# GpSimd DRAINs in the conditional expert blocks, and x's four buffers moved to 256 bytes (modulo 512) from the weights

## The chip, the core and the metric

The kernel runs on one NeuronCore of a Trainium2 chip. The metric is the device time in microseconds of one execution; the median of three runs is compared. Engines are named as the profile names them: PE is TensorE's matmuls, PEld its weight loads, DVE is VectorE, ACT is ScalarE, POOL is GpSimd, SP is SyncE; a q behind a name (POOLq) marks an instruction that the engine's sequencer runs by itself.

## The reference, cut to what matters

Three stages follow each other on 4608 tokens of 512 features.

```
attn:  8 heads, chunks of 64 tokens: softmax(q k^T / 8) v        -> x    (4608 x 512)
moe:   h = max(x@w1, x@w2, x@w3);  x2 = h @ w_out                 FF 768
moe2:  e = argmax(x2 @ w_gate) for each token, 8 experts
       out = prob(e) * sigmoid(x2 @ w_output_gate)[e] * (relu(x2 @ w1[e]) @ w2[e])   FF 1024
```

All is float32; each product of the dense parts is done as three matmuls of high and low parts (hi·hi, hi·lo, lo·hi).

## The kernel before, in words

**Attention and the dense layer.** The 36 tiles of 128 tokens are cut into nine blocks of four tiles (512 tokens). A planner (`add`, `order`) writes out by hand in which order each engine's instructions stand. Attention of the next block fills the gaps of the current block's dense layer. Attention leaves x transposed, split into a high and a low half, in `xt[j % 2]`: even blocks use the buffers `xth0` and `xtl0`, odd blocks `xth1` and `xtl1`, each 128 partitions of 4·512 floats (8192 bytes). `moe_f` (18 calls a block) multiplies: a weight piece of 128x128 from `wpc` is the stationary operand, 512 columns of `xt` stream past it; `mm3` is the three matmuls, lines 102 (hi, hi), 103 (hi, lo) and 104 (lo, hi), so a block has 18·4·3 = 216 such matmuls. `moe_y` then has `ht` as the stationary and `wo` as the moving operand (256 or 272 columns). `gate` ranks the tokens by expert, and `rows_out` writes x2 to a scratch tensor in HBM.

**The expert stage.** Tokens of one expert are taken in blocks of 256. `step(b)` does one block: `gather_ahead(b + 2)` (POOL: `places`, then two indirect DMAs that gather 128 rows each into `xg`), first layer (`l1_mm`: stationary `wpc`, 256 moving columns of `xs`), the transposes of the next block (`x_T`), second layer (`l2_mm`: stationary `wo`'s `hT`, 512 moving columns of `wpc`), and for each half `y_act` on ACT and `y_out`, an indirect DMA on POOL that scatters 128 rows to the output. Where the next block has another expert, `switch` loads and splits new weights. Blocks 0 to 17 always run; `tail` puts blocks 18 to 25 into nested conditions (`tc.If(total > b)`), since how many are needed depends on the routing. With these inputs blocks 18, 19 and 20 run and 21 to 25 do not. Line 1192 is the condition, and what an engine does at it where the block is left out; line 1232 is the close of the whole program; line 1212 its start.

**Where the buffers lie.** A pool hands out addresses in the order in which its tags are first asked for. In pool `p1` the six small `mx` and `sm` buffers (32 bytes a partition each) come first, then the slots of `xth0`, `xtl0`, `xth1`, `xtl1`, then `ht0` to `ht5`, `hs0`, `U` and the small gate buffers. A slot is as large as the largest tile that uses it: `xth1`'s slot is later used for `xg01` (2·2·516 floats, 8256 bytes), `xtl1`'s slot for `xs0`, `ht`'s slots for `yo`. The pool `wp` with the weights (`wpc` pieces of 16384 and 8192 bytes, then `wo`) stands ahead of `p1`. Within the expert stage `hT` and the odd blocks' `xs` lie in `wo`, at multiples of 512 bytes from the weights.

Of the kernel before, what the change touches and what calls it, by code (L numbers as in the profile page):

```python
# [10 lines left out]
F32 = mybir.dt.float32  # L11
# [10 lines left out]
def tile_chunk_attention_moe_moe(  # L22
# [16 lines left out]
    PE, ACT, DVE, POOL, SP = nc.tensor, nc.scalar, nc.vector, nc.gpsimd, nc.sync  # L39
# [7 lines left out]
    P = 128  # L47
# [5 lines left out]
    XW = DM + 4  # L53
# [3 lines left out]
    NB0 = NT // BP  # L57
# [108 lines left out]
    p1 = ctx.enter_context(tc.tile_pool(name="p1", bufs=1))  # L166

    def buf(shape, dtype, name):
        return p1.tile(shape, dtype, name=name, tag=name)
# [10 lines left out]
    pTF = [part(3, i, 1).rearrange("p (a c i) -> p a c i", a=HP, c=2) for i in range(2)]  # L180
    NV = len(v_buf)
    mxs, sms = ([buf([P, H], F32, f"{n}{i}") for i in range(NE2)] for n in ("mx", "sm"))
    XN = KD * TB * P
    xtn = lambda hl, i: f"xt{'hl'[hl]}{i}"
    xtile = lambda hl, i: p1.tile([P, KD, TB * P], F32R, name=xtn(hl, i), tag=xtn(hl, i))
# [559 lines left out]
    NX = 3  # L745
# [16 lines left out]
    lastx = (NB - 1) % 2  # L762

    def xkeys(i, *hls):
        return [("xt", i, t, hl, h2) for t in range(TB) for hl in hls for h2 in range(2)]
# [5 lines left out]
        [("pTF", i) for i in range(2)] + [("cy", i) for i in range(2)],  # L771
    ]
    raw = [Late(ar, f"R{n}", [P, 4, DM], F32, f"raw{n}", akeys[n]) for n in range(4)]
    xg01 = Late(p1, xtn(0, 1 - lastx), [P, 2, 2, XW], F32, "xg01",
                xkeys(1 - lastx, 0) + [("xg", i, t) for i in range(2) for t in range(2)])
    xs0 = Late(p1, xtn(1, 1 - lastx), [P, 2, KD, BP], F32R, "xs0", xkeys(1 - lastx, 1) + [("xs0", i) for i in range(4)])
    xg2 = Late(wp, f"P{NFT // 4}", [P, 2, XW], F32, "xg2", [("w", n, hl) for n in range(16, NFT) for hl in range(2)])
    S2 = Late(p1, xtn(0, lastx), [P, XN], I32, "S2", xkeys(lastx, 0) + ["S2"])
    yol = [Late(p1, f"ht{i}", [P, DM], F32, f"yo{i}", [("ht", i, 0), ("ht", i, 1)]) for i in range(4)]
# [21 lines left out]
    ]  # L801
    xsk = [[("xs0", i) for i in range(4)], [("wo", i) for i in range(8, 12)]]
    hTk = [("wo", i) for i in range(8)]
    xg = lambda b: xg2.t if b % NX == 2 else xg01.t[:, b % NX]
    yo = lambda b, t: yol[2 * (b % 2) + t].t
    bk = [("mm", 0), ("mm", 1), ("mm", 2), ("mm", 0)]
    ps_x = ps_a2.rearrange("p (a b) -> p a b", a=KD)
# [11 lines left out]
    def sval(engines, row, b, hi):  # L819
        return nc.values_load(  # L820
            sched_i()[0:1, row * NBLK + b:row * NBLK + b + 1], engines=engines, min_val=0, max_val=hi
        )
# [7 lines left out]
    def gather(b, t, rows=NT):  # L830
        POOL.indirect_dma_start(  # L831
            out=xg(b)[:, t], out_offset=None, in_=x2d[0:rows, :],
            in_offset=bass.IndirectOffsetOnAxis(ap=ic[b % 4]()[:, t, 0:1].bitcast(U32), axis=0),
        )

    def places(b):
        cv = sval([ET.Pool], 0, b, NCOL - 2)
        POOL.tensor_copy(ic[b % 4](), idx()[:, bass.ds(cv, 2), :])  # L838
# [18 lines left out]
    def l1_mm(b, c, i):  # L857
        x, ps = xs[b % 2](), l1_ps(c)
        w, ff = wx[c // 2], ((2 * c + i) % 4) * P
        for kk in range(KD):  # L860
            mm3(
                ps[:, i], w[:, 0, kk, ff:ff + P], w[:, 1, kk, ff:ff + P], x[:, 0, kk], x[:, 1, kk],
                kk == 0, kk == KD - 1,
            )

    def l1_hi(c):
        ACT.activation(out=hT()[:, 0, 2 * c:2 * c + 2], in_=l1_ps(c), func=ACTF.Relu)  # L867

    def l1_lo(c):
        fs = slice(2 * c, 2 * c + 2)  # L870
        DVE.scalar_tensor_tensor(  # L871
            out=hT()[:, 1, fs], in0=l1_ps(c), scalar=0.0, in1=f(hT()[:, 0, fs]), op0=ALU.max, op1=ALU.subtract
        )
# [235 lines left out]
    def x_T(b):  # L1109
        if b < NBLK:  # L1110
            xT_mm(b)
            for i in range(2):
                xT_hi(b, i)
                xT_lo(b, i)

    def switch(b, ns):


        lv, cl, en = meta[b]
        with tc.If(lv > 0):  # L1120
            for n in ns:
                for kk in range(4):
                    conv_hi(n, kk)
                    conv_lo(n, kk)
        for n in ns:
            load_x(n, en, cl)

    def scalars(b):
        meta[b] = (
            sval([ET.Activation, ET.DVE], 1, b, 1), sval([ET.SP], 2, b, 1), sval([ET.SP], 3, b, E - 1)  # L1130
        )

    def gather_ahead(b):
        if b < NBLK:
            places(b)
            for t in range(2):
                gather(b, t)

    def l2(b, t):
        for ff in range(2 * KD):  # L1140
            l2_mm(t, ff)
        if t == 0:
            y(b, t)

    def y(b, t):
        y_act(b, t)
        y_out(b, t)

    def step(b):
        scalars(b)  # L1150
        gather_ahead(b + 2)
        for c in range(4):
            for i in range(2):
                l1_mm(b, c, i)
            l1_hi(c)
            l1_lo(c)
            if c == 2:
                switch(b, (0,))
        x_T(b + 1)
        switch(b, (1,))  # L1160
        if b + 1 < NBLK:
            full[b + 1] = sval([ET.PE], 7, b + 1, 1)
        l2(b, 0)
        with tc.If(full[b] > 0):
            l2(b, 1)
        y(b, 1)
        switch(b, (2, 3))
# [17 lines left out]
    for b in range(1, NB0):  # L1185
        step(b)
    total = sval(None, 6, 0, NBLK)

    def tail(b):
        if b == NBLK:  # L1190
            return
        with tc.If(total > b):  # L1192
            step(b)
            tail(b + 1)
# [42 lines left out]
```

## Time and profile before

| | |
|---|---|
| median of three runs | 1209.3 us (1208.03 to 1210.64) |
| the profiled execution | 1207.82 us, span 1206.0 us from the first to the last instruction |
| PE busy | 1181.2 us, 98% of the span |
| DVE, ACT, POOL busy | 436.7, 418.1, 195.7 us |
| granted TensorE clock | 0.995 of full speed over the span |

Busy time is a share of the span; matmuls are pipelined and their ends modelled, so a busy PE may still run at different rates. The rate is read from start to start of matmuls that follow each other. Sequencer instructions (branches, semaphore waits, DRAIN) do not count as busy and stand in the view of a source line alone.

### The profile page before, as it was taken

What the parts mean: (1) busy time and instruction counts of PE and PEld (TensorE: products, weight loads), DVE (VectorE), ACT (ScalarE), POOL (GpSimd) and SP (SyncE); (2) the same over time, 40 slices, a digit from 0 to 9 for tenths busy, and PEclk for the clock granted to TensorE, in tenths of its full rate; (3) what the DMA queues carried; (4) which work ended last, traced back from release to release, by engine and by line L of the source; (5) the groups of instructions that cost most, each with busy time, mean ns of one, the idle gap of its engine ahead of it and who ended that gap; (6) DMA issues with size and microseconds to landing.
All of it is one profiled execution on the core that took longest, in us unless ns stands there. A gap on an engine that the chain in (4) does not pass through costs nothing. (4 is left out here: it accounts for less than half of the span.)

```text
span 1206.0 us, 23510 instructions
## 1 busy us (share of the span) xinstructions
PE 1181.2 (98%) x9219; PEld 1035.3 (86%) x9219; DVE 436.7 (36%) x1095; ACT 418.1 (35%) x1192; POOL 195.7 (16%) x243
## 2 busy tenths in 40 slices
PE   7999999999999999999999999999999999999995
PEld 6879788897888988988879898989989989999994
DVE  7995413232232322322323452211266211511270
ACT  5575323333243332333322322212256212512271
POOL 1000111111211111111111112112112212112120
PEclk9999999999999999999999999999999999999998
DMA  8842212121121121211230015111156211511151
GB/s 283 245 140 71 86 30 87 47 58 59 35 80 53 47 69 36 80 54 35 73 106 36 1 45 201 54 45 53 46 207 241 100 44 48 180 45 62 38 171 29
DMA packets 84318, 103.06 MB, mean 85 GB/s; under 512 B 40287, under 2 KB 49503, under 8 KB 84192
## 3 DMA queue, kind: packets, MB, share of 16 engines
q1 hardware_dynamic: 77152, 79.82, 20.7%
q0 software_dynamic: 7040, 21.60, 5.6%
q8 instruction: 75, 1.23, 0.4%
q14 instruction: 51, 0.42, 0.1%
HBM read 149.55 MB, written 20.52 MB: 141 GB/s over the span
## 5 line engine op out<-in xcount | busy, mean ns | idle before, releaser
L102 PE MATMUL mm<-xth,wpc 128*128 128x512 f32 x576 | 233.8, 406 | 0.0
L104 PE MATMUL mm<-xth,wpc 128*128 128x512 f32 x576 | 226.5, 393 | 0.0
L103 PE MATMUL mm<-xtl,wpc 128*128 128x512 f32 x576 | 226.0, 392 | 0.1
L613 DVE TENSOR_TENSOR hs<-mm,hs 128x512 f32<-128x512 f32 x108 | 74.4, 688 | 184.0 <-PE mm L104 184.0
L871 DVE SCALAR_TENSOR_TENSOR wo<-mm,wo 128x512 fp32r<-128x512 f32 x64 | 43.5, 689 | 239.1 <-ACT wo L867 208.6
L104 PEld LDWEIGHTS mm<-xth,wpc 128*128 128x128 f32 x576 | 108.3, 188 | 24.7
L102 PEld LDWEIGHTS mm<-xth,wpc 128*128 128x128 f32 x576 | 108.2, 188 | 23.8
L103 PEld LDWEIGHTS mm<-xtl,wpc 128*128 128x128 f32 x576 | 108.5, 188 | 21.3 <-DVE xtl L99 0.4
L102 PE MATMUL mm<-wo,ht 128*128 128x256 f32 (+1 forms) x432 | 126.2, 292 | 0.0
L104 PE MATMUL mm<-wo,ht 128*128 128x256 f32 (+1 forms) x432 | 122.7, 284 | 0.0
L103 PE MATMUL mm<-wo,ht 128*128 128x256 f32 (+1 forms) x432 | 122.6, 284 | 0.0
L102 PE MATMUL tr<-wpc,wo 128*128 128x512 f32 x304 | 120.3, 396 | 0.0
L104 PE MATMUL tr<-wpc,wo 128*128 128x512 f32 x304 | 118.5, 390 | 0.0
L103 PE MATMUL tr<-wpc,wo 128*128 128x512 f32 x304 | 118.3, 389 | 0.0
L99 POOL TENSOR_TENSOR ht<-hs,ht 128x512 fp32r<-128x512 f32 x48 | 62.0, 1291 | 293.2 <-ACT ht L615 293.2
L887 POOL DMA_INDIRECT out_dram<-yo,S x42 | 43.7, 1042 | 355.2 <-ACT yo L884 271.4
L615 ACT CAST ht<-hs 128x512 fp32r<-128x512 f32 x54 | 33.6, 623 | 160.9 <-DVE hs L613 160.8
L459 ACT ACTIVATE rg<-a,mx 128x64 f32<-128x64 f32 x264 | 78.7, 324 | 22.1 <-DVE mx L453 22.1
L99 DVE TENSOR_TENSOR wpc<-raw,wpc 128x512 fp32r<-128x512 f32 x112 | 70.2, 684 | 39.8 <-ACT wpc L825 39.8
L102 PEld LDWEIGHTS mm<-wo,ht 128*128 128x128 f32 x432 | 81.2, 188 | 1.8 <-issue 0.4
L103 PEld LDWEIGHTS mm<-wo,ht 128*128 128x128 f32 x432 | 81.5, 189 | 0.4
L104 PEld LDWEIGHTS mm<-wo,ht 128*128 128x128 f32 x432 | 81.3, 188 | 0.0
(243 smaller groups left out, 2258.3 us busy)
## 6 DMA issues: line engine op xcount, KB each, us to landing
raw<-in_moe_w_dram SPq DMA_DIRECT2D x92, 1024.0 KB
x_scratch<-U SPq DMA_DIRECT2D x36, 258.0 KB
rg<-in_q_dram SPq DMA_DIRECT2D x36, 256.0 KB
rg<-in_k_dram SPq DMA_DIRECT2D x36, 256.0 KB
wst<-in_moe_w_dram SPq DMA_DIRECT2D x18, 512.0 KB
rg<-in_v_dram SPq DMA_DIRECT2D x128, 64.0 KB
U<-in_moe_w_out_dram SPq DMA_DIRECT2D x6, 512.0 KB
rg<-in_v_dram SPq DMA_DIRECT2D x4, 256.0 KB
```

What stands on the lines that cost most here:

```text
L99: eng.tensor_tensor(out=o, in0=a, in1=b, op=ALU.subtract)
L102: PE.matmul(o, ah, bh, start=first, stop=False)
L103: PE.matmul(o, ah, bl, start=False, stop=False)
L104: PE.matmul(o, al, bh, start=False, stop=last)
L459: ACT.activation(out=ex[:, b, hp], in_=bank[b][:, hp], func=ACTF.Exp, scale=scale, bias=mx[:, HP * b + hp:HP * b + hp + 1], accum_out=sm[: ...
L613: add("DVE", t_dve(N), up, [pk, hk], [hk], lambda: DVE.tensor_tensor(out=h, in0=ps, in1=h, op=ALU.max))
L615: add("ACT", t_act(N), up, [hk], [("ht", g, 0)], lambda: ACT.copy(ht[g][:, 0, :N], h))
L871: DVE.scalar_tensor_tensor(out=hT()[:, 1, fs], in0=l1_ps(c), scalar=0.0, in1=f(hT()[:, 0, fs]), op0=ALU.max, op1=ALU.subtract)
L887: POOL.indirect_dma_start(out=out, out_offset=bass.IndirectOffsetOnAxis(ap=ic[b % 4]()[:, t, 1:2].bitcast(U32), axis=0), in_=yo(b, t), in_ ...
```

## The change

Three edits. A `drain` of the GpSimd is put into `step`, behind the gathers and ahead of the first layer, for blocks 18 and up. A new buffer of 48 floats (192 bytes a partition) that nothing uses is asked for ahead of `xth0`, which moves everything behind it in `p1`. And the rows of `xg01` become 544 floats long, of which 516 are used as before, so that its slot has 2·2·544·4 = 8704 bytes instead of 8256.

```diff
     mxs, sms = ([buf([P, H], F32, f"{n}{i}") for i in range(NE2)] for n in ("mx", "sm"))
+
+    buf([P, 48], F32, "pad")
     XN = KD * TB * P
...
-    xg01 = Late(p1, xtn(0, 1 - lastx), [P, 2, 2, XW], F32, "xg01",
+    xg01 = Late(p1, xtn(0, 1 - lastx), [P, 2, 2, 544], F32, "xg01",
                 xkeys(1 - lastx, 0) + [("xg", i, t) for i in range(2) for t in range(2)])
...
-    xg = lambda b: xg2.t if b % NX == 2 else xg01.t[:, b % NX]
+    xg = lambda b: xg2.t if b % NX == 2 else xg01.t[:, b % NX, :, 0:XW]
...
     def step(b):
         scalars(b)
         gather_ahead(b + 2)
+        if b >= NB0:
+            POOL.drain()
         for c in range(4):
             for i in range(2):
                 l1_mm(b, c, i)
```

## Rows read from the trace of the kernel before

**Rows 1.** The page's first part: busy us, share of the span, instructions.

```profile
PE 1181.2 (98%) x9219; PEld 1035.3 (86%) x9219; DVE 436.7 (36%) x1095; ACT 418.1 (35%) x1192; POOL 195.7 (16%) x243
```

**Rows 2.** Timelines of ACT and POOL, last rows: start us, us, instruction, idle before.

```profile
1191.82 0.69 ACT L884 ACTIVATE yo<-tr,xg 128x512 f32<-128x512 f32 x1 [4.75 <-PE tr L104]
...
1192.78 1.00 POOL L887 DMA_INDIRECT out_dram<-yo,S  x1 [4.42 <-ACTq L1120]
```

**Rows 3.** View of line 1192: count, ns min/median/max, first and last start us.

```profile
L1192 POOLq EVENT_SEMAPHORE  x6: 17/30/43, 1193.0 to 1195.7; - x6
L1192 POOLq COMPARE_BRANCH  x5: 34/38/50, 1132.8 to 1197.8; - x5
L1192 POOLq INC_SWDGE_SEM  x1: 1960/1960/1960, 1195.8 to 1195.8; - x1
```

**Rows 4.** View of line 1232, the close, POOL and SP.

```profile
L1232 SPq EVENT_SEMAPHORE  x14: 17/28/28, 1197.7 to 1206.0; - x14
L1232 POOLq DRAIN  x3: 46/107/7261, 1197.9 to 1205.7; - x3
L1232 SPq DRAIN  x3: 7/7/13, 1198.4 to 1205.4; - x3
```

**Rows 5.** View of line 1212, the start, POOL.

```profile
L1212 POOLq INC_SWDGE_SEM  x1: 31/31/31, 0.2 to 0.2; - x1
L1212 POOLq DRAIN  x1: 184/184/184, 0.4 to 0.4; - x1
```

**Rows 6.** Views of lines 887 (scatters) and 831 (gathers): all POOL DMAs.

```profile
L887 POOL DMA_INDIRECT out_dram<-yo,S x42: 997/1015/1442, 740.5 to 1192.8; - x42
...
L831 POOL DMA_INDIRECT xg<-x_scratch,S x46: 942/993/1466, 704.7 to 1176.0; - x46
DMA to landing us min/median/max: 3.2/3.7/6.4
```

**Rows 7.** POOL's timeline: the first scatter of blocks 18, 19 and 20.

```profile
1150.59 1.02 POOL L887 DMA_INDIRECT out_dram<-yo,S  x1 [13.85 <-ACT yo L884]
...
1169.03 1.01 POOL L887 DMA_INDIRECT out_dram<-yo,S  x1 [9.06 <-ACT yo L884]
...
1187.34 1.01 POOL L887 DMA_INDIRECT out_dram<-yo,S  x1 [10.40 <-ACT yo L884]
```

**Rows 8.** Windows of one odd and one even dense block: length, PE busy.

```profile
271.60:348.20 76.60, 76.60 (x640) 1.00 0.20 57
348.20:424.30 76.10, 76.10 (x640) 1.00 0.19 57
```

**Rows 9.** PE timeline, dense matmuls of an even block, ends of 37 unbroken rows.

```profile
376.76 0.39 PE L103 MATMUL mm<-xtl,wpc 128*128 128x512 f32 x1
...
385.01 0.39 PE L103 MATMUL mm<-xtl,wpc 128*128 128x512 f32 x1
```

**Rows 10.** The same of an odd block, ends of 37 unbroken rows.

```profile
453.04 0.39 PE L103 MATMUL mm<-xtl,wpc 128*128 128x512 f32 x1
...
461.39 0.39 PE L103 MATMUL mm<-xtl,wpc 128*128 128x512 f32 x1
```

**Rows 11.** PE timeline, second layer of an expert block, ends of 46 rows.

```profile
758.24 0.39 PE L103 MATMUL tr<-wpc,wo 128*128 128x512 f32 x1
...
768.46 0.39 PE L103 MATMUL tr<-wpc,wo 128*128 128x512 f32 x1
```

**Rows 12.** PE timeline, first layer, blocks 1 (wo) and 2 (xs): ends of 95 rows each.

```profile
745.62 0.28 PE L102 MATMUL mm<-wo,wpc 128*128 128x256 f32 x1
...
756.89 0.28 PE L103 MATMUL psg<-wo,wpc 128*128 128x256 f32 x1
...
768.92 0.28 PE L102 MATMUL mm<-xs,wpc 128*128 128x256 f32 x1
...
780.19 0.28 PE L103 MATMUL psg<-xs,wpc 128*128 128x256 f32 x1
```

## The prediction, made before the changed kernel was run

> **What bounds the kernel now.** I read the page's busy shares first: PE is busy 98% of the span, every other engine under 40% [rows 1]. So the time is PE's instruction stream, plus the tail that starts when PE has no more to do. Two places remain where this change can act: how fast matmuls follow each other, and that tail.
>
> The tail, next, from the timelines of ACT and POOL and from the views of lines 1192 and 1232. ACT scales the last output half at 1191.82, POOL starts its scatter at 1192.78 [rows 2]. POOL then goes through the skipped condition: its semaphore waits are over at 1195.7, INC_SWDGE_SEM takes 1.96 us from 1195.8, the branch is at 1197.8 [rows 3]. A DRAIN starts at 1197.9 and the longest of the three takes 7.26 us; SP, which waits for the same semaphores, goes from 1197.7 to its DRAINs at 1198.4 [rows 4]. So from about 1198.5 on four engines wait for one POOL instruction that computes nothing. After it some 0.8 us of barrier are left to 1206.0.
>
> The matmul rate, last, by start to start. In an even block 36 steps take 385.01 − 376.76 = 8.25 us, 229.2 ns each [rows 9]; in an odd block 8.35 us, 231.9 ns [rows 10]. Whole blocks say the same: 76.6 us odd, 76.1 even, equal counts of instructions, PE never idle [rows 8]. The expert stage's 512-column matmuls take 10.22 us for 45 steps, 227.1 ns [rows 11].
>
> **The DRAINs.** At 1197.9 nothing is in flight on POOL: the waits for all its DMAs' semaphores ended at 1195.7 [rows 3]. At the program's start, with no DMA issued, a DRAIN takes 0.18 us and an INC_SWDGE_SEM 0.03 [rows 5]; the close's other two DRAINs, right behind the long one, take at most 0.11 [rows 4]. Between lie 42 scatters and 46 gathers, 88 indirect DMAs, and no other DRAIN [rows 6]. I read the 7.26 us as work left over by finished DMAs: (7.26 − 0.18) / 88 = 80 ns each. INC_SWDGE_SEM looks like the same, (1.96 − 0.03) / 88 = 22 ns each.
>
> By that reading the new DRAIN in block 18 clears 42 gathers and 36 scatters, 78 · 0.08 + 0.2 = 6.5 us; those in blocks 19 and 20 find four DMAs each, 0.5 us. Each may also wait for the gathers just ahead of it, whose landing takes 3.7 us from issue (median) [rows 6]. What is queued behind it on POOL is the block's first scatter; ACT writes that `yo` buffer again two blocks later, so only then does anything wait for it. POOL idles 13.85, 9.06 and 10.40 us before these scatters [rows 7]: 6.5 plus some 2.7 left of the landing fits into 13.85, 0.5 + 2.7 into the others. Cost of the three: nothing. Were each to take 7.26 + 2.7 = 10.0 us, block 19's scatter would be 0.9 us late, and no matmul waits for it.
>
> At the close two scatters are left, so DRAIN takes 0.18 + 2 · 0.08 = 0.34 us (6.9 less), INC_SWDGE_SEM some 0.25 instead of 1.96 (1.7 less; for its eight semaphores I allow more than 0.03 + 2 · 0.022). What is late next is SP: it starts when INC_SWDGE_SEM ends, about 1196.05, and needs its 0.75 us to 1196.8, where POOL would be done at 1196.6. So 0.2 to 0.3 us come back: −8.3 us. Bounds: 0, if the DRAIN's time is not of finished DMAs, and −8.6. I take −8.3, since the start and the two later DRAINs are the nearest rows.
>
> On DRAIN the Trainium skill, "PSUM — Partial Sum Buffer", Engine vs sequencer instructions, says that a drain waits until its engine is fully idle. By that alone a DRAIN in block 18 takes over nothing from the one at the close, and the time is that of the first rival below. The trace does not fit it well: the engine had no work left and the DRAIN still took 7.26 us.
>
> **The addresses.** The pad is 192 bytes and is to make the distance 256, so `xth0`, `xtl0` and `xth1` lie 64 bytes (modulo 512) from the weights now. `xth1`'s slot has 8256 = 16 · 512 + 64 bytes, so `xtl1` lies at 128. With slots of 8704 = 17 · 512 bytes all four come to 256. That odd and even blocks differ in nothing else that I can name, and by 2.7 ns a matmul, says that addresses count. In the second layer moving and stationary operand are at distance 0, at 227.1 ns.
>
> No row shows a dense matmul at 256. What I can say of it: high and low part are at one distance again, as in even blocks. So I take the even blocks' 229.2 ns for all nine: 4 odd blocks · 216 · 2.7 ns = 2.3 us by the unbroken runs, 4 · 0.5 = 2.0 us by whole blocks [rows 8]; I use −2.2. Bounds from rows, however far: at distance 0's 227.1 it is 5 · 216 · 2.1 + 4 · 216 · 4.8 = −6.4 us; if 256 is as much worse than 64 as the steps seen so far continue (2.7 ns for each of three further steps of 64 bytes, 237.3 ns), it is 1944 · 237.3 = 461.3 against now 1080 · 229.2 + 864 · 231.9 = 447.9, +13.4 us.
>
> `xs0` moves from 128 to 256 from the weights. Its first layer now takes (780.19 − 768.92) / 94 = 119.9 ns a matmul, that with `xs` in `wo`, at distance 0, (756.89 − 745.62) / 94 = 119.9 [rows 12]. So distance does nothing at 256 columns, and I cost this at 0, as `moe_y`, whose pairs of `ht` and `wo` rows lie at several distances before and after. Gathered rows of 544 floats carry the same bytes; they are hidden two blocks ahead.
>
> On this the Trainium skill, "TensorE: Matmul & The Clock Gate", Part 2: What happens when you issue a matmul, says that PE has two independent SBUF read ports, so that loading the next weights takes nothing from the running matmul. By that addresses do nothing, and the time is the third rival's. Odd and even blocks in this trace differ, 76.6 against 76.1 us, which speaks against it.
>
> **The sum.** −8.3 − 2.2 = −10.5 us. The profiled execution's 1207.82 (span 1206.0 and 1.8 around it) becomes 1197.3. It lies 1.5 under the median of 1209.3, so the median becomes **1198.8**. From run to run this kernel shows about 0.2% (2.4 us); less than that I call the same.
>
> **The rivals.**
> - *The close's DRAIN keeps its 7.26 us* (a fixed price, or one of the whole program's history that an earlier DRAIN doesn't clear). For it: no row shows a DRAIN with DMAs behind it other than this one. Against it: the three short ones. Then only the addresses count: 1209.3 − 2.2 = 1207.1. Chance 12%.
> - *256 is as good as 0*: −8.3 − 6.4 = −14.7, 1194.6. For it: at distance 0 the same width runs at 227.1 ns; if distances are alike that lie half a period apart, 256 is one of the good ones. Against it: nothing measures it. 20%.
> - *Addresses do nothing*, and odd blocks are slow for another reason, such as their neighbours in the planner's order: 1209.3 − 8.3 = 1201.0. 12%.
> - *Slower: the rate gets worse with distance.* 0, 64 and 64 with 128 give 227.1, 229.2 and 231.9 ns, a rise without a turn so far. Going on to 237.3 ns it costs 13.4 us in the dense blocks and eats the tail's gain: 1209.3 − 8.3 + 13.4 = 1214.4. It decides from (447.9 + 8.3 us) / 1944 = 234.7 ns a matmul. Against it: the first layer shows no such rise between 0 and 128. 8%.
>
> **Chances and range.** The forecast has 45% (1196.5 to 1201.5 by itself), the rivals 20, 12, 12 and 8; 3% for something else. Faster by over 0.2%: the forecast, the second and third rival, and some 6 of the first's 12 (it stands just at the bound), 83%. Within 0.2%: the other 6 and half of the slower rival, whose size is anyone's guess, with a little of the rest, 12%. Slower: 5%. The range from 1193.5 to 1206.5 leaves out most of the first and the slower rival and what would be a gain beyond distance 0.
>
> **What would show it.** The view of line 1232 should have no POOL DRAIN over 1 us, that of line 1192 an INC_SWDGE_SEM well under 1 us, and a new DRAIN of some 6 to 9 us should stand in block 18, with short ones in 19 and 20. The span behind the last ACT row should be some 6 us instead of 14.2. Dense blocks should all take 76.1 us, and unbroken runs 229 ns. I am wrong if a DRAIN of 7 us still closes the program, or if the blocks' length goes over 77.3 us (234.7 ns), or if a matmul waits for a scatter or `yo` in blocks 18 to 20.

## The result, and the profile after

| | before | changed |
|---|---|---|
| median of 6 runs | 1209.44 us (1208.03 to 1210.64) | 1196.96 us (1193.98 to 1197.63) |
| ratio | | 0.9892, 95% interval 0.9879 to 0.9905 |
| profiled execution, span | 1207.82, 1206.0 us | 1197.1, 1195.4 us |

By the medians the change is worth 12.5 us, where 10.5 were forecast: 1196.96 us against 1198.8. (The median before stands on six runs here, three more than ahead of the prediction.)

PE's busy time fell by 1.8 us and the span by 10.6, so in the profiled executions most of the gain lies where PE has no work [rows 1].

```profile
PE 1179.4 (99%) x9219; PEld 1037.5 (87%) x9219; DVE 436.9 (37%) x1095; ACT 417.7 (35%) x1192; POOL 195.8 (16%) x243
```

The tail, by the timelines of ACT and POOL. The last `y_act` starts 2.38 us earlier than before [rows 2]. From there to the end of the span it is 1195.4 − 1189.44 = 6.0 us, before 14.2.

```profile
1189.44 0.69 ACT L886 ACTIVATE yo<-tr,xg 128x512 f32<-128x512 f32 x1 [4.75 <-PE tr L104]
...
1190.40 1.00 POOL L889 DMA_INDIRECT out_dram<-yo,S  x1 [4.42 <-ACTq L1122]
```

The views of the condition (L1196, before L1192 [rows 3]), of the close (L1236, before L1232 [rows 4]) and of the new DRAIN (L1155). Columns as in the groups named. INC_SWDGE_SEM went from 1960 to 231 ns, the close's longest DRAIN from 7261 to 212 ns. SP's DRAINs now start behind the end of POOL's first (1194.0 + 0.21): SP is late next. The three new DRAINs are long.

```profile
L1196 POOLq INC_SWDGE_SEM  x1: 231/231/231, 1193.6 to 1193.6; - x1
...
L1236 POOLq DRAIN  x3: 46/107/212, 1194.0 to 1195.1; - x3
L1236 SPq DRAIN  x3: 7/7/13, 1194.5 to 1194.8; - x3
...
L1155 POOLq DRAIN  x3: 5379/7060/8416, 1132.3 to 1172.3; - x3
```

They cost nothing. The first scatter of blocks 18, 19 and 20 waits for ACT's `yo` after the same idle times as before [rows 7]. PE's waits from 1125 us on, in the last of these views (what it waited for, us, times, longest), are 0.6 us for its own branches, as before, and for no scatter or `yo`.

```profile
1148.09 1.02 POOL L889 DMA_INDIRECT out_dram<-yo,S  x1 [13.85 <-ACT yo L886]
...
1166.52 1.01 POOL L889 DMA_INDIRECT out_dram<-yo,S  x1 [9.04 <-ACT yo L886]
...
1184.97 1.01 POOL L889 DMA_INDIRECT out_dram<-yo,S  x1 [10.54 <-ACT yo L886]
```

```profile
PE mm L102 <- PEq L1168: 0.6, 2, 0.3
```

The dense blocks, by windows (length, PE busy and so on): one odd and one even block, both 75.80 us, where before the odd one took 76.6 and the even one 76.1 [rows 8].

```profile
272.38:348.18 75.80, 75.80 (x641) 64.41 (x640) 22.57 (x71) 25.10 (x98) 12.32 (x14) 1.00 0.19 57
348.18:423.98 75.80, 75.80 (x641) 64.42 (x640) 22.57 (x71) 25.11 (x98) 12.41 (x14) 1.00 0.19 57
```

PE's timeline, the ends of an unbroken run of 38 rows (37 steps) in an odd block and in an even one: 327.68 − 319.26 = 403.48 − 395.06 = 8.42 us, 227.6 ns a step; by the trace's nanoseconds 227.3. Before, such runs took 231.9 ns in odd and 229.2 ns in even blocks [rows 9, 10]. The pad moves `ht` too, but the gain is not there: step by step, odd block 3 gains 0.81 us between one dense matmul and the next, and nothing (−0.01 us) inside `moe_y`. Last, the first layer out of `xs0`: 95 steps in 11.39 us, 119.9 ns, as in [rows 12].

```profile
319.26 0.39 PE L103 MATMUL mm<-xtl,wpc 128*128 128x512 f32 x1
...
327.68 0.39 PE L104 MATMUL mm<-xth,wpcr 128*128 128x512 f32 x1
...
395.06 0.39 PE L103 MATMUL mm<-xtl,wpc 128*128 128x512 f32 x1
...
403.48 0.39 PE L104 MATMUL mm<-xth,wpcr 128*128 128x512 f32 x1
...
812.89 0.28 PE L102 MATMUL mm<-xs,wpc 128*128 128x256 f32 x1
...
824.28 0.28 PE L104 MATMUL psg<-xs,wpc 128*128 128x256 f32 x1
```

One thing must be known before executions are compared to a microsecond. Where block 1's first dense matmul stands differs, in the 14 profiles of this study, between 117.9 and 120.7 us, with either addresses. The granted clock goes with it in part. The changed kernel's profiled execution had two stretches of 3.4 us at the lower level (1.2 GHz), at 26.8 and 84.8 us; the kernel before had none. (No such stretch gave 117.9 and 118.1 us and three gave 120.7, but profiles with a single one lie anywhere from 118.0 to 120.5.) Windows (last columns: granted clock, DMA share, GB/s), first of the changed kernel:

```profile
16.00:20.00 4.00, 2.16 (x94) 1.94 (x95) 2.61 (x7) 2.55 (x6) 0.00 (x0) 1.00 1.07 366
20.00:32.00 12.00, 10.17 (x202) 9.26 (x198) 10.75 (x25) 8.13 (x27) 0.00 (x0) 0.86 0.84 244
...
64.00:92.00 28.00, 27.04 (x221) 22.27 (x220) 26.25 (x58) 18.50 (x50) 0.00 (x0) 0.94 0.40 123
```

and of the kernel before:

```profile
16.00:20.00 4.00, 1.45 (x69) 1.22 (x70) 3.06 (x8) 2.66 (x6) 0.00 (x0) 1.00 1.07 365
20.00:32.00 12.00, 10.03 (x224) 8.79 (x224) 11.11 (x27) 8.14 (x27) 0.00 (x0) 1.00 0.85 251
...
64.00:92.00 28.00, 27.05 (x229) 22.42 (x228) 27.30 (x62) 19.30 (x51) 0.00 (x0) 1.00 0.40 123
```

From 16 to 20 us PE was busy for 2.16 us in the changed kernel and for only 1.45 in the kernel before, where the clock stayed up, so these rows don't tell why it fell. Below, "from block 1 on" is the profiled time less that start, which takes this out: 1207.82 − 118.08 = 1089.7 us before, 1197.1 − 119.69 = 1077.4 us changed, 12.3 us less, 8.2 of them in the tail. Some us behind the last matmul the clock falls in every profile; nothing there is PE's. The first matmul of block 1, before, changed, and with the addresses alone:

```profile
118.08 0.40 PE L102 MATMUL mm<-xth,wpc 128*128 128x512 f32 x1
```
```profile
119.69 0.40 PE L102 MATMUL mm<-xth,wpc 128*128 128x512 f32 x1
```
```profile
120.69 0.40 PE L102 MATMUL mm<-xth,wpc 128*128 128x512 f32 x1
```

### The profile page after: what moved, and what is told of

It is laid out like the page before. It is cut to its first block, busy times and chain, and to the rows that moved or that the text cites. A ratio compares the mean times of both kernels' runs of the same rounds, so it can differ in the third digit from the quotient of the medians.

```text
span 1195.4 us, 23513 instructions
## 1 busy us (share of the span) xinstructions
PE 1179.4 (99%) x9219; PEld 1037.5 (87%) x9219; DVE 436.9 (37%) x1095; ACT 417.7 (35%) x1192; POOL 195.8 (16%) x243
## 5 line engine op out<-in xcount | busy, mean ns | idle before, releaser
L102 PE MATMUL tr<-wpc,wo 128*128 128x512 f32 x304 | 120.4, 396 | 0.0
L102 PEld LDWEIGHTS mm<-wo,ht 128*128 128x128 f32 x432 | 81.3, 188 | 1.7 <-issue 0.4
L103 PEld LDWEIGHTS mm<-wo,ht 128*128 128x128 f32 x432 | 81.5, 189 | 0.4
L869 ACT ACTIVATE wo<-mm 128x512 fp32r<-128x512 f32 x64 | 38.1, 597 | 124.8 <-PE mm L104 121.7
```

The source lines that it names most:

```text
L102: PE.matmul(o, ah, bh, start=first, stop=False)
L103: PE.matmul(o, ah, bl, start=False, stop=False)
```

## The experiments

All runs ran in three batches, each on a chip of its own and beside the kernel before (medians 1208.88, 1209.38 and 1209.82 us). Gains and ratios are against the kernel before of the same batch; "from block 1 on" is against the profiled execution shown above.

**The DRAINs alone.**

```diff
+        if b >= NB0:
+            POOL.drain()
```

> The three DRAINs alone, every buffer where it was before. Theory (DRAIN works off finished indirect DMAs and waits for the gathers just ahead of it): the close's DRAIN about 0.2 us, the new ones as in the changed kernel (8.4, 7.1 and 5.4 us), dense blocks as before (76.6 odd, 76.1 even), time 8.3 us below the kernel before, about 1201.1. Rival (the gain of the changed kernel is mostly the addresses' and part of the tail's was given back elsewhere): less than 7 us.

1200.13 us, 8.75 less, ratio 0.9931 (0.9918 to 0.9945); from block 1 on 1081.4 us, 8.4 less. Dense blocks take 76.6 and 76.1 us as before. The close, where the longest DRAIN is as short as in the changed kernel:

```profile
L1234 POOLq DRAIN  x3: 46/107/212, 1196.1 to 1197.2; - x3
```

The theory's size holds, the rival is out.

**The addresses alone** (pad and rows of 544 floats, no DRAIN).

> The addresses alone, no DRAIN added. Theory (256 is as good as 0): each dense block 75.8 us instead of 76.6 (odd) and 76.1 (even), so 4 x 0.8 + 5 x 0.3 = 4.7 us less, about 1204.7; the close's DRAIN 7.3 and INC_SWDGE_SEM 2.0 us as before. Rival (the forecast's size): 2.2 us less, 1207.2. Rival (the 1.6 us by which block 1 starts later in the changed kernel's profile belongs to the addresses and not to that one execution): 3.1 us less, 1206.3, with block 1 again near 119.7 us.

1205.79 us, 3.1 less, ratio 0.9968 (0.9956 to 0.9979); from block 1 on 1085.4 us, 4.4 less. The profiled execution had three stretches at the lower clock ahead of block 1, which began at 120.7 us. Dense blocks take 75.8 us, the close's DRAIN 7.26 us and INC_SWDGE_SEM 1.96 as before:

```profile
273.27:349.07 75.80, 75.80 (x641) 64.42 (x639) 22.56 (x71) 25.10 (x98) 12.32 (x14) 1.00 0.20 57
```
```profile
L1194 POOLq INC_SWDGE_SEM  x1: 1960/1960/1960, 1194.0 to 1194.0; - x1
L1234 POOLq DRAIN  x3: 46/107/7261, 1196.2 to 1204.0; - x3
```

From block 1 on the two parts nearly add up: 8.4 + 4.4 against 12.3. So from there on the addresses are worth twice what was forecast. The median, 3.1 us less, is what the last rival expected, that the addresses make block 1 late; but block 1 also began at 120.1 and 120.4 us with the old addresses (the two block-10 kernels below) and at 118.2 and 118.4 with x at 256 (the last two kernels). So the late start comes and goes with the execution, and no run ties it to the addresses.

**One DRAIN, in block 18; one, in block 10.**

```diff
+        if b == NB0:          # the other kernel: b == 10
+            POOL.drain()
```

> One DRAIN, in block 18 alone; addresses as before. It leaves the DMAs behind it to the close: 4 gathers (for blocks 21 and 22) and 6 scatters, 10 in all. Theory (80 ns for each finished indirect DMA): the close's DRAIN 0.18 + 10 x 0.08 = 1.0 us, time about 7.5 us below before, 1201.9. Rival (a DRAIN is long only when it is the first of the program): 0.2 us, 8.3 us below. Rival (an earlier DRAIN clears nothing): 7.3 us, no gain.

> One DRAIN, in block 10 alone, which always runs; addresses as before. Ahead of it lie 26 gathers and 20 scatters, behind it 20 gathers and 22 scatters. Theory (80 ns each): the DRAIN in block 10 takes 46 x 0.08 + 0.2 = 3.9 us behind the second gather's issue or until the gathers have landed, whichever is later; the close's takes 0.18 + 42 x 0.08 = 3.5 us and INC_SWDGE_SEM about half of 1.96; time some 4.6 us below before, 1204.8. Rival (first of the program alone is long): the close's DRAIN 0.2 us, 8.3 us below. Rival (what counts is the time since the last DRAIN, or nothing is cleared): 7.3 us, no gain.

1201.28 us (0.9942, 0.9928 to 0.9955) and 1204.75 us (0.9968, 0.9956 to 0.998), both as the price per DMA has it. INC_SWDGE_SEM, the close and the new DRAIN, with the DRAIN in block 18:

```profile
L1194 POOLq INC_SWDGE_SEM  x1: 391/391/391, 1195.7 to 1195.7; - x1
L1234 POOLq DRAIN  x3: 46/107/874, 1196.2 to 1197.7; - x3
L1153 POOLq DRAIN  x1: 8406/8406/8406, 1134.7 to 1134.7; - x1
```

and in block 10:

```profile
L1194 POOLq INC_SWDGE_SEM  x1: 1031/1031/1031, 1197.6 to 1197.6; - x1
L1234 POOLq DRAIN  x3: 52/107/3492, 1198.8 to 1202.9; - x3
L1153 POOLq DRAIN  x1: 8414/8414/8414, 955.1 to 955.1; - x1
```

With 2, 10, 42 and 88 DMAs since the last DRAIN the close's takes 0.21, 0.87, 3.49 and 7.26 us: (7.261 − 0.212) / 86 = 82 ns each and 0.05 fixed. INC_SWDGE_SEM takes 0.23, 0.39, 1.03 and 1.96 us: 20 ns each and 0.19 fixed. "Only the first is long", "nothing is cleared" and "the time since the last DRAIN counts" are out: the last two expected 7.3 us at the close. Each of these DMAs moves 128 rows, so a price per DMA and one per row or packet are not told apart. But block 10's DRAIN took 8.41 us with 46 DMAs behind it, as long as block 18's with 78, and 3.9 us were expected. So two more runs.

**One DRAIN, in block 10 ahead of the gathers; one, in block 20 behind them.**

```diff
+        if b == 10:
+            POOL.drain()
         gather_ahead(b + 2)
+        if b == NB0 + 2:      # the other kernel, this one alone
+            POOL.drain()
```

> The kernel before with one DRAIN in block 10, ahead of that block's gathers instead of behind them. With the DRAIN behind them it ended 6.44 us after the second gather's issue although only 46 DMAs lay behind it, as long as in block 18 with 78. Theory (82 ns for each finished DMA, and what is longer is the wait for the gathers to land and to be worked off): 44 x 0.082 = 3.6 us behind the last scatter's issue or some tenths after its landing, whichever is later; close 44 x 0.082 + 0.05 = 3.7 us. Rival (the program's first DRAIN with DMAs behind it takes some 6.4 us whatever their number): 6.4 us again.

> The kernel before with one DRAIN, in block 20 alone, behind the gathers: 86 DMAs, two scatters left for the close. Theory (82 ns each from the second gather's issue): 86 x 0.082 = 7.05 us behind that issue; the close 0.21 us, time as with three DRAINs. Rival (a first DRAIN has a fixed length): 6.45 us behind the issue, the close 0.21 us all the same. Block 20's first scatter is due 10.4 us after the gathers, so nothing should come late.

One time each: 1205.26 and 1200.14 us. Ahead of the gathers, in block 10:

```profile
L1152 POOLq DRAIN  x1: 4919/4919/4919, 953.4 to 953.4; - x1
L1234 POOLq DRAIN  x3: 52/107/3660, 1199.1 to 1203.3; - x3
```
```profile
953.63 1.00 POOL L887 DMA_INDIRECT out_dram<-yo,S  x1 [4.42 <-ACTq L1120]
```

and in block 20:

```profile
L1153 POOLq DRAIN  x1: 9247/9247/9247, 1175.8 to 1175.8; - x1
L1234 POOLq DRAIN  x3: 46/107/217, 1196.9 to 1198.1; - x3
```
```profile
1176.99 0.97 POOL L831 DMA_INDIRECT xg<-x_scratch,S  x1 [0.31 <-issue]
```

A DRAIN's record begins while POOL still issues the DMAs ahead of it, whose last issue is the second view of each pair, so its length is counted here from the end of that issue (ends by the trace's nanoseconds). Block 10, ahead of the gathers: the last scatter's issue ended at 954.64, the DRAIN at 958.32, 3.68 us for 44 DMAs, 84 ns each. Block 20: from 1177.96 to 1185.07, 7.11 us for 86, 83 ns each; block 18 6.46 us for 78. The fixed first price is out. The new DRAINs of blocks 19 and 20 in the changed kernel had four DMAs each; there the gathers' packets set the end: the last ones ended at 1161.77 and 1177.10 (from the packets' records), the DRAINs at 1162.55 and 1177.66. Block 10 with the DRAIN behind the gathers remains: 6.44 us from the last issue, 2.38 from the last packet, where 46 DMAs are worth 3.8 from the issue. Some of the working off seems to stand behind the gathers' landing there, and not in block 18; why, no run tells.

**x at other distances.** The changed kernel with other pads; 0 by asking for the last two `sm` buffers behind `ht`.

```diff
-    buf([P, 48], F32, "pad")
+    buf([P, 16], F32, "pad")   # 128; 192: 32 floats; 64: no pad
```

> All four parts of x 64 bytes (modulo 512) from the weights, DRAINs as in the changed kernel. Theory A (128 is a bad distance, and the odd blocks were slow because their low part lay there): all blocks as the even ones of before, 76.1 us, unbroken runs 229.2 ns. Theory B (a block is slow because its high and low part lie at different distances): also 76.1 us, this run does not tell the two apart, the next does. Time: the changed kernel's plus 9 x 0.3 = 2.7 us, about 1199.5. Rival (distance does nothing, odd blocks differ by their neighbours): odd blocks stay at 76.6.

> All four at 128. Theory A (128 is bad): each block at or over 76.6 us, unbroken runs 231.9 ns or more (only the low part lay at 128 before, one matmul in three); if the low part's matmuls alone made the odd blocks 2.7 ns slower on average, 229.2 + 3 x 2.7 = 237 ns, 77.8 us a block, 18 us over the changed kernel. Theory B (unequal distances are bad): no slower than at 64, 76.1 us or less, at most 2.7 us over the changed kernel.

> All four at 192. If the rate falls again on the way from 128 to 256, or only unequal distances hurt: between 75.8 and 76.1 us a block, 227.3 to 229.2 ns. If what counts repeats every 256 bytes and is alike on both sides, 192 is as 64: 229.2 ns. If only 0 and 256 are good and the rest is worse the further from both: worst at 128, 192 again 229.2.

> All four at 0 (the pad left out and five of the six small buffers' last two asked for behind ht, so that what lies ahead of x is 64 bytes shorter). Theory (0 and 256 are alike): 75.8 us a block, unbroken runs 227.1 to 227.4 ns, the changed kernel's time within 1 us. Rival (the expert stage's 227.1 ns at 0 was that stage's, not the distance's; both operands starting in the same place collide): dense blocks slower than at 256.

Windows of dense block 3, each from its first matmul to the next block's: at 0, then at 64, 128 and 192.

```profile
272.12:347.90 75.78, 75.78 (x640) 64.37 (x639) 22.56 (x71) 25.15 (x98) 12.41 (x14) 1.00 0.20 58
```
```profile
271.84:347.89 76.05, 76.05 (x641) 64.40 (x639) 22.56 (x71) 25.14 (x98) 12.36 (x14) 1.00 0.19 57
```
```profile
274.83:351.57 76.74, 76.74 (x640) 64.46 (x639) 22.55 (x71) 25.14 (x98) 12.35 (x14) 1.00 0.20 58
```
```profile
273.33:350.26 76.93, 76.93 (x640) 64.50 (x639) 22.55 (x71) 25.14 (x98) 12.36 (x14) 1.00 0.19 56
```

| x from the weights, modulo 512 | 0 | 64 | 128 | 192 | 256 |
|---|---|---|---|---|---|
| dense, 512 columns, unbroken run, ns | 227.3 | 229.2 | 233.1 | 233.4 | 227.3 |
| first layer out of `xs0`, 256 columns, unbroken run, ns | 119.9 | 117.8 | 119.9 | 117.8 | 119.9 |
| median time, us | 1196.20 | 1196.09 | 1205.06 | 1202.79 | 1196.96 |
| 95% interval of the ratio to before | .988–.991 | .9881–.9911 | .9951–.9978 | .994–.9968 | .9879–.9905 |

Odd and even blocks are alike in every column, so "distance does nothing" is out. In the dense blocks the rate gets worse from 0 to 192 and is back at 256. Theory A's direction holds, its 237 ns do not; theory B (only unequal distances hurt) falls at 128. At 192 none of the three expectations, 227.3 to 229.2 ns, came. No expectation had the second line: at 64 and 192 the first layer is 2.1 ns a matmul faster, and 11 blocks · 96 matmuls · 2.1 = 2.2 us. That is why 64 is no slower than 256 (9 · 0.25 = 2.3 us lost in the dense blocks). The rows at 812.89 to 824.28 above have their answer at 64 and at 192:

```profile
813.59 0.28 PE L102 MATMUL mm<-xs,wpc 128*128 128x256 f32 x1
...
824.78 0.28 PE L104 MATMUL psg<-xs,wpc 128*128 128x256 f32 x1
```
```profile
820.39 0.28 PE L102 MATMUL mm<-xs,wpc 128*128 128x256 f32 x1
...
831.58 0.28 PE L104 MATMUL psg<-xs,wpc 128*128 128x256 f32 x1
```

11.19 us instead of 11.39 for the same 95 steps.

In this sweep the weights never moved, so x's own address would explain the table as well as the distance. `moe_y` tells more: there `wo` moves past and lay in one place in every kernel, and only the stationary `ht` went along with the pad. Its unbroken runs of 53 steps at 272 columns take 6.61 to 6.65 us in all kernels of the sweep, but which steps are long depends on where `ht` lies: the mean of each step agrees within 0.3 ns with `ht` at 0 and at 256, and differs by up to 10 ns between 0 and 64. So the stationary operand's place counts too, and it also repeats after 256 bytes.

**Each at its best distance.** The changed kernel with `xs0` alone moved to 320; then the odd blocks' `xs` in `wo` from 0 to 64 too. (`xs0`'s larger slot also moves `ht` by 64 bytes.)

```diff
-    xs0 = Late(..., [P, 2, KD, BP], ...
+    xs0 = Late(..., [P, 2 * KD * BP + 16], ...
-        lambda: xs0.t,
+        lambda: xs0.t[:, 16:].rearrange("p (a k n) -> p a k n", a=2, k=KD),
-        lambda: wo_t[0]...[:, 4096:6144]...
+        lambda: wo_t[0]...[:, 4112:6160]...     # the second kernel only
```

> The changed kernel, with xs0 alone moved 64 bytes further, to 320 from the weights; x stays at 256. In the sweep the first layer out of xs0 took 119.9 ns a matmul at 0 and 256 and 119.6 at 128, but 117.8 at 64 and 117.3 at 192, while the dense matmuls of 512 columns had 0 and 256 as their best. Theory (the rate at 256 columns depends on the distance too, by another rule, which repeats every 256 bytes): 117.8 ns, 11 blocks x 96 matmuls x 2.0 ns = 2.1 us under the changed kernel, about 1194.9, dense blocks still 75.8 us. Rival (in the runs at 64 and 192 the first layer was faster for what x's own move did): 119.9 ns, no gain. Rival (no repeat): any rate between 117 and 122 ns.

> As the run before, and the odd blocks' xs inside wo moved 64 bytes too, from distance 0 to 64. Theory: both first layers at 117.8 ns, another 10 x 96 x 2.1 = 2.0 us, about 1193 and the fastest of all. Rival (xs in wo has another reason for its 119.9 ns): as the run before.

1193.73 us (0.9873, 0.9858 to 0.9888) and 1191.41 us (0.985, 0.9837 to 0.9864). The second is the fastest of all, 18.4 us under the kernel before, and its interval lies under the changed kernel's. From block 1 on: 1074.7 and 1072.5 us against 1077.4. Both first layers of the second kernel, blocks 4 and 5, 95 steps in 11.19 us:

```profile
810.25 0.28 PE L102 MATMUL mm<-xs,wpc 128*128 128x256 f32 x1
...
821.44 0.28 PE L104 MATMUL psg<-xs,wpc 128*128 128x256 f32 x1
...
833.36 0.28 PE L102 MATMUL mm<-wo,wpc 128*128 128x256 f32 x1
...
844.55 0.28 PE L104 MATMUL psg<-wo,wpc 128*128 128x256 f32 x1
```

The dense blocks stay at 227.3 ns. At 256 columns 320 gives the same 117.8 ns as 64. So the first layer's gain came from where `xs` lies, and the repeat after 256 bytes holds at the points tried: 0 and 256, 64 and 320. (`moe_y`, whose `ht` also came to 320 in these two kernels, has the steps of the kernel at 64 within 3 ns.)

## Why the prediction was right, and where it was not

- **DRAIN as work left over by finished DMAs: right.** 80 ns a DMA were read from one row, 82 came out over five counts; INC_SWDGE_SEM 22 forecast, 20 measured. The tail gave 8.2 us in the profile (14.2 to 6.0) and 8.4 with the DRAINs alone (from block 1 on; 8.75 by the medians), for −8.3.
- **SP late next: right.** POOL's first DRAIN ends at 1194.2, SP's starts at 1194.5.
- **The new DRAINs cost nothing: right, though two lengths were wrong.** 0.5 us and some landing were forecast for blocks 19 and 20; they take 7.06 and 5.38, because the record begins 2 us before the second gather's issue is through and the packets take until 4.3 and 2.7 us after that. Block 20's 5.4 us still fit into 10.4 of idle time.
- **The addresses: the direction right, the size half.** The step that failed is "So I take the even blocks' 229.2 ns for all nine". At 256 they run at 227.3, as the rival "256 is as good as 0" had it. That rival's −6.4 us was too much: it put the unbroken runs' difference on all 216 matmuls, while the whole blocks gain less than that (0.8 us where 216 · 4.8 ns make 1.04). By whole blocks it is 4 · 0.8 + 5 · 0.3 = 4.7 us, of which 4 · 0.8 + 4 · 0.3 = 4.4 lie from block 1 on, where 4.4 were measured. The median fell between forecast and rival, 1.8 us below the one and 2.4 above the other. That the profiled execution came out at 1197.1 us, where 1197.3 were forecast, is luck: its block 1 began 1.6 us later than in the execution before, which hid most of the missing 2.2 us.
- **"Distance does nothing at 256 columns": wrong.** It rested on 0 and 128 alone, which with 256 are the three slow places of the table (119.9 ns each). `xs0`'s move from 128 to 256 cost 0.3 us over all eleven blocks, by their first and last rows, so the term was small; the reason was false and hid the 4.9 us (from block 1 on) that the last kernel gained over the changed one.
- **"The rate gets worse with distance": half right.** It does, up to 192 and to 233.4 ns, and then turns. 64 bytes less of pad, x at 192, cost 9 · 1.13 = 10 us in the dense blocks against the changed kernel, of which the faster first layer gave 2.2 back; by the medians it was 5.8.
- **The Trainium skill, "TensorE: Matmul & The Clock Gate", Part 2: What happens when you issue a matmul** (loading weights takes nothing from the running matmul): five distances with the same instructions differ by 6 ns of 227, so what the prediction drew from it, that addresses do nothing, is wrong here. Whether the weight load is what costs the 6 ns, and so whether the sentence itself fails, no run shows: every matmul in these kernels has a weight load of its own.
- **The Trainium skill, "PSUM — Partial Sum Buffer", Engine vs sequencer instructions** (a drain waits for an idle engine): not against the trace, where a DRAIN ends behind the issues ahead of it and, in blocks 19 and 20, 0.8 and 0.6 us behind the gathers' last packets; but at the close the engine had nothing left, and the 82 ns for each finished DMA come on top.

## What to carry to other kernels

Where a program ends on a GpSimd DRAIN, count the indirect DMAs since the last one; here a DRAIN in an idle stretch of POOL, as late as it could be hidden, took their price out of the tail. Matmuls that each load their own weights differed here by 2 to 3% in rate by where moving operand and weights lie modulo 256 bytes, and the good place for 512 columns was a bad one for 256: read the rate start to start for each width, at more than two distances, before an address is called indifferent. Two points that agree show no rule when both may lie on the same side of a period.

## What the runs showed of the hardware that was not expected

- DRAIN on POOL: 82 ns for each indirect DMA since the last DRAIN (2, 10, 42, 44 and 88 of them: 0.21, 0.87, 3.49, 3.66 and 7.26 us), INC_SWDGE_SEM 20 ns each.
- PE's rate against the operands' distance: 227.3 to 233.4 ns at 512 columns, 117.8 to 119.9 ns at 256. At 64, against 0, 512 columns lose 1.9 ns and 256 columns gain 2.1; 0 and 256, and for 256 columns 64 and 320, are alike. In `moe_y` the stationary operand's move alone changes which steps are long.
- The granted clock's stretches of 3.4 us at the lower level (1.2 GHz) in the first 90 us of most profiled executions, none to three of them, with either addresses.
- Open: why a DRAIN with 46 DMAs behind freshly issued gathers took 6.44 us from the last issue, why block 1 begins up to 2.8 us later in some executions, and why the rate follows the distance as it does.
